# Loading q and k in runs of 32 features and transposing them on the vector engine, in a top-k attention with an MLP behind it

## The chip, the core and the metric

The kernel runs on one core of a Trainium2 chip. Its engines run side by side, each through its own queue in order: PE (TensorE, matmuls and transposes; PEld is its weight load), DVE (VectorE), ACT (ScalarE), POOL (GpSimd) and SP, which only issues DMAs here. The metric is the device time of one execution in microseconds, as the median of several runs. Lower is better.

## The reference

Eight batches of eight heads, 576 rows, 64 features: scores of every query against every key, of which only the 32 largest of a row are kept for a softmax; the result times v. The heads of one row side by side are the input x (4608 x 512) of an MLP with an exact GELU.

```python
scores = (1/sqrt(64)) * q @ k.T                   # per batch and head, 576 x 576
kth    = 32nd largest of each row
scores = where(scores >= kth, scores, -1e9)
attn   = exp(scores - max); attn /= attn.sum() + 1e-9
x      = (attn @ v) as (8*576, 8*64)
out    = gelu(x @ w_in) @ w_out                   # 512 -> 2048 -> 512
```

## The kernel before

**Pairs and items.** Two heads form a pair (`NP` = 4 pairs a batch, 32 in all). A pair's 576 rows are four blocks of 128 rows (`NM` = 4, `SM` = 512) and a tail of 64 (`TL`). An item is one block of a pair, both heads, or the tails of two pairs: 18 items a batch, 144 in all, in the order of the list `items`. The main loop `for n in range(ahead)` takes one step for each item and is written as a software pipeline by hand: in step n the scores of item n+2 are computed (`scores`), the largest 32 of item n are searched on DVE (`top_k`), the softmax of item n-1 runs on ACT (`softmax`), the probabilities of item n-2 are transposed on PE (`transposes`) and those of item n-3 multiplied by v (`attend`). The order of the text is the order of each engine's queue; nothing reorders it.

**A step on DVE.** `top_k` is eight MAX8 (line 344) and six MATCH_REPLACE8 (line 347) over 128 x 576. Then stands the hook `inverse(n - 1)`, the reciprocal of the softmax sums of the item before (line 370). It waits for `add_small` on POOL (line 376), which waits for the two softmax passes of ACT (lines 383, 384). Behind the reciprocal, POOL's `normalise` (line 396) scales the rows, and PE's `transposes` of that item (lines 415 to 433) come in the next step. In five steps around step 14 DVE takes over `normalise`.

**MLP.** Its matmuls (lines 522 and 558) are cut into pieces; a step takes at most eight (`left[0]`), from step `START` = 10 on. What is left runs behind the last item. Before `START`, `keep_busy` (line 636) fills PE with matmuls that nobody reads, and the weights (fp64 in memory) are loaded and converted unit by unit, one unit a step (`load_weights` on SP, `weights_size` on ACT, `weights_add` on POOL).

**q and k.** Scores need q and k with features on the partitions. `load` (lines 84 to 95) brings rows onto partitions: for each tensor of a pair two DMAs of 128 x 4 x 64 and two of 64 x 64, in runs of 64 features, 256 bytes. They go to SP's queue, but for k of pair 0 (ACT's and POOL's). There are two buffers for q and two for k. `transpose_qk` turns a pair: ten 128 x 128 transposes on PE (line 246) in three pieces of four, two and four, each piece into one PSUM tile `tp_qk` and from there by one copy on ACT into the tile `qk` (line 250; two of pair 0's copies are on DVE). The last piece issues the loads of the pair after next into the buffers that have come free. `slots_of` and `first` say in which step, counted from a batch's first, each piece of a pair is put; the pieces stand among PE's transposes and MLP pieces there. Pairs 0 and 1 are turned before the loop.

A tile `qk` holds q in columns 0 to 767 (512, then the tails of both heads on the diagonal of a block with zeros, then the same for k) and k behind them. There are six such buffers.

Of the kernel before, what the change touches and what calls it, by code (L numbers as in the profile page):

```python
# [14 lines left out]
def kernel(  # L15
# [52 lines left out]
    xT = const.tile([P, KO, RING], f32, name="xT")  # L68


    raws = {n: [const.tile([P, NJ, 2, D], f32, name=f"raw_{n}{i}") for i in range(m)]
            for n, m in (("k", 2), ("q", 2), ("v", NP + 1))}
    nc.gpsimd.memset(raws["k"][0][:, NM], 0.0)
    for t in raws["v"][:1] + raws["q"] + raws["k"][1:] + raws["v"][1:]:
        nc.vector.memset(t[:, NM], 0.0)


# [3 lines left out]
    def raw_of(n, pair):  # L81
        return raws[n][pair % len(raws[n])]

    def load(n, pair, queue=None, queue2=None):
        if pair >= n_pairs:
            return
        queue = queue or nc.sync
        queue2 = queue2 or queue
        b, h0 = pair // NP, 2 * (pair % NP)
        t, src = raw_of(n, pair), sources[n]  # L90
        for e in range(2):
            queue.dma_start(
                out=t[:, 0:NM, e, :], in_=src[b, h0 + e, 0:SM].rearrange("(t p) d -> p t d", p=P)
            )
            queue2.dma_start(out=t[e * TL : (e + 1) * TL, NM, e, :], in_=src[b, h0 + e, SM:S])

    load("k", 0, nc.scalar, nc.gpsimd)
    load("q", 0)
    make_identity(nc, ident)

# [127 lines left out]
    N = len(items)  # L228


    KT = SM + 2 * P
    qk_of = {}

    def transpose_qk(pair, first=False):

        rq, rk = raw_of("q", pair), raw_of("k", pair)
        blocks = [(rq, j) for j in range(NJ)] + [(rk, NM)] + [(rk, j) for j in range(NM)]

        def piece(c, n):
            if pair not in qk_of:  # L240
                qk_of[pair] = work.tile([P, KT + SM], f32, tag="qk", bufs=NP + 2, name="qk")
            t = qk_of[pair]
            tp = ps.tile([P, 512], f32, tag="tp", name="tp_qk")
            for x in range(n):
                r, j = blocks[c + x]
                nc.tensor.transpose(  # L246
                    tp[:, x * P : (x + 1) * P], r[:, j].rearrange("p e d -> p (e d)"), ident
                )
            copy = nc.vector.tensor_copy if first and c > 0 else nc.scalar.copy
            copy(out=t[:, c * P : (c + n) * P], in_=tp[:, 0 : n * P])  # L250
            if c == 0:
                load("q", pair + 2)
                load("k", pair + 2)

        return [lambda c=c, n=n: piece(c, n) for c, n in ((6, 4), (4, 2), (0, 4))]

# [18 lines left out]
    def scores(i):  # L277
        if i >= N:
            return
        pair, t = items[i]  # L280
        S_of[i] = s = work.tile([P, 2 * S], f32, tag="s", bufs=5, name="s")
        s_ps = ps.tile([P, 2, 512], f32, tag="s", bufs=1, name="s_ps")
        t_ps = ps.tile([P, 512], f32, tag="tp", name="t_ps")
        if t < NM:
            qk = qk_of[pair]
            lhsT = qk[:, t * P : (t + 1) * P]
            nc.tensor.matmul(t_ps[:, 0:P], lhsT=lhsT, rhs=qk[:, SM + P : KT], start=True, stop=True)  # L287
            for c in range(2):
                for e in range(2):
                    rows = slice(e * D, (e + 1) * D)  # L290
                    nc.tensor.matmul(  # L291
                        s_ps[:, e, c * 256 : (c + 1) * 256], lhsT=lhsT[rows, :],
                        rhs=qk[rows, KT + c * 256 : KT + (c + 1) * 256], start=True, stop=True,
                    )
            if i == 0:

                nc.scalar.activation(s[:, 0:SM], s_ps[:, 0], func=AF.Copy, scale=scale)  # L297
                nc.vector.tensor_scalar(s[:, SM : S + TL], t_ps[:, 0:P], scale, None, op0=ALU.mult)
                nc.scalar.activation(s[:, S + TL :], s_ps[:, 1], func=AF.Copy, scale=scale)  # L299
                return  # L300
            nc.scalar.activation(spread(s, S + TL, SM), s_ps, func=AF.Copy, scale=scale)  # L301
            nc.scalar.activation(s[:, SM : S + TL], t_ps[:, 0:P], func=AF.Copy, scale=scale)
        else:
            for r in range(2):
                qk = qk_of[pair + r]
                for e in range(2):
                    nc.tensor.matmul(
                        t_ps[half(r, e), r * TL : (r + 1) * TL],
                        lhsT=qk[:, SM + e * TL : SM + (e + 1) * TL],
                        rhs=qk[:, SM + P + e * TL : SM + P + (e + 1) * TL],  # L310
                        start=True, stop=True,
                    )

            for r in range(2):
                qk = qk_of[pair + r]
                for e in range(2):
                    rows = slice(e * D, (e + 1) * D)
                    nc.tensor.matmul(  # L318
                        s_ps[half(r, e), r, :], lhsT=qk[rows, SM + e * TL : SM + (e + 1) * TL],
                        rhs=qk[rows, KT:], start=True, stop=True,  # L320
                    )
            s2 = s.rearrange("p (r n) -> p r n", r=2)
            nc.scalar.activation(s2[:, :, 0:SM], s_ps, func=AF.Copy, scale=scale)
            nc.scalar.activation(
                s2[:, :, SM:S], t_ps[:, 0:P].rearrange("p (r n) -> p r n", r=2),
                func=AF.Copy, scale=scale,
            )
# [309 lines left out]

    keep_busy(WARM, idle)
    for pair in range(2):
        for piece in transpose_qk(pair, pair == 0):  # L640
            piece()
        if pair == 0:
            scores(0)
            scores(1)
# [1 line left out]


    slots_of = [
        [(-8, -7, -6), (-5, -4, -3), (-2, -1, 0), (1, 2, 3)],
        [(-10, -9, -8), (-7, -6, -5), (-4, -4, -3), (-3, -2, -2)],  # L650
    ]
    first = {2: (0, 1, 1), 3: (2, 2, 3)}
    prep_in = {}
    for pair in range(2, n_pairs):
        b, p = divmod(pair, NP)
# [3 lines left out]
    for n in range(ahead):  # L659

        left[0] = 4 if n in (START, START + 1) else 8
        eager[0] = n > N
        if not waits(unit_in(n)):
            weights_add(unit_in(n))
        scores(n + 2)
        product = attend(n - 3)
        late = n > START
        if n <= START:

            softmax(n - 1, 0)  # L670
        copy_x()
        if waits(unit_in(n)):
            weights_size(unit_in(n))
            weights_add(unit_in(n))
        mlp(1)
        tr = transposes(n - 2)
        if product and n > START and done[0] < len(pieces) and pieces[done[0]][0] > ready[0]:

            for piece in tr[:1]:
                piece()  # L680
            tr, ready[0] = tr[1:], n_tok[0]
        if n > START:
            softmax(n - 1, 0)
        mlp(1)
        if not late:
            softmax(n - 1, 1)
        mlp(1)
        if n < START:

            keep_busy((4 if product or n == 0 else 14) * (1 if n < 5 else 2), ident)  # L690
        prep = prep_in.pop(n, [])
        if n == START + 1:

            for piece in prep:
                piece()
            prep = []
        if len(prep) > 1 and len(tr) == 3:
            tr, prep = tr[:1] + prep[:1] + tr[1:], prep[1:]
        for piece in tr[:-1]:
            piece()  # L700
            if n < START and product and piece is tr[0]:
                keep_busy(5 if n < 5 else 10, ident)
            ready[0] = n_tok[0]
            mlp(1)
        ready[0] = n_tok[0]
        if late:
            softmax(n - 1, 1)
        add_small(n - 1)
        if ends_late(unit_in(n)):
            weights_end(unit_in(n))  # L710
        for piece in tr[-1:] + prep:
            piece()
            mlp(1)
        if n == 1:
            keep_busy(8, ident)

        run_gelus()
        mlp(left[0])
        run_gelus()
        if n < N:  # L720
            top_k(n, {3: lambda: inverse(n - 1)})
        else:
            inverse(n - 1)
        threshold(n)
        u = unit_in(n + 1)

        normalise(n - 1, 2 if on_pool(u) else 0)

        if not waits(unit_in(n + 1)):
            weights_size(unit_in(n + 1))  # L730
        for m in (n + 1, n + 2):

            if m > 2 and waits(unit_in(m)) == (m == n + 1):
                load_weights(m)
        if n <= NP:
            load("v", n)
# [38 lines left out]
```

## Time and profile before

| what | before |
|---|---|
| time, median of 3 runs (lowest, highest) | 1637.5 us (1636.53, 1637.75) |
| profiled execution: span from first to last instruction | 1634.7 us; what lies around it is not in the profile |
| PE / weight loads busy | 1611.5 / 1105.8 us |
| DVE / ACT / POOL busy | 1414.9 / 1185.3 / 665.3 us |
| mean granted TensorE clock | 0.999 |
| matmuls of `tp_qk` | 320, in the chain of work that ended last 2% |
| copies of `tp_qk` on ACT | 94, 48.3 us |
| idle time of DVE before the reciprocal | 134.4 us in 86 waits |
| idle time of DVE at the end | 73.7 us |
| DMA packets | 126768, of which 117776 under 512 bytes |
| load of q, 128 KB, issue to landing | 2.4 us (median of 64) |

Busy time is the time in which an engine worked on at least one instruction. In the lists of groups a line reads: source line, engine, operation, tile written and tiles read, shapes, count, then busy time in us and mean duration of one in ns, then the idle time of the engine just before them and what ended it. A mean duration on PE is longer than the distance from one matmul to the next, since matmuls overlap. In the table by stage each engine has its busy time and, in brackets, its instructions, and the last three columns are the granted clock, the busy share of the 16 DMA engines and GB/s.

### The profile page before, as it was taken

To read this page: it belongs to the slowest core of one execution; us is meant where nothing else is said; L and a number is where in the kernel's file an instruction comes from. 1 tells how busy PE (TensorE), PEld (TensorE's weight loads), DVE (VectorE), ACT (ScalarE), POOL (GpSimd) and SP (SyncE) were. 2 spreads that over 40 slices of the span, in tenths; PEclk is the share of its full clock that TensorE was granted. 3 is DMA by queue.
4 is the path that set the end of the run, shared out by engine and by line. 5 is a ranking of instruction groups with operands and counts; after the bars stand their busy time and mean duration, and the time that the engine had idled before them with its cause. 6 is when DMAs were issued, how large, how long until landed. Compare 5 with 4: busy or idle time off the path is not lost.

```text
span 1634.7 us, 25758 instructions
## 1 busy us (share of the span) xinstructions
PE 1611.5 (99%) x9184; PEld 1105.8 (68%) x9184; DVE 1414.9 (87%) x3046; ACT 1185.3 (73%) x2132; POOL 665.3 (41%) x760
## 2 busy tenths in 40 slices
PE   7999999999999999999999999999999999999999
PEld 5776676766666666666666667676666666666665
DVE  8999999988898899998899899998889889999800
ACT  6989877777777777777777777777777777777720
POOL 4986833333333333333333333333333333333300
PEclk9999999999999999999999999999999999999999
DMA  6523210011101120001110111001110101000000
GB/s 165 157 76 117 81 43 1 14 40 33 36 1 28 30 58 1 14 19 33 29 28 15 28 30 43 1 14 36 37 36 1 28 16 36 1 14 4 4 14 13
DMA packets 126768, 56.19 MB, mean 34 GB/s; under 512 B 117776, under 2 KB 118064, under 8 KB 126640
## 3 DMA queue, kind: packets, MB, share of 16 engines
q1 hardware_dynamic: 125376, 54.12, 12.3%
q8 instruction: 73, 1.20, 0.3%
q10 hardware_dynamic: 1200, 0.39, 0.1%
q14 instruction: 55, 0.45, 0.1%
q0 software_dynamic: 64, 0.03, 0.0%
HBM read 45.08 MB, written 9.44 MB: 33 GB/s over the span
## 4 chain that ended last, share of the span: by engine, by line
PE 91%; DVE 5%; ACT 2%; POOL 1%; issue 0%; SPq 0%; DMA 0%; DVEq 0%; POOLq 0%; ACTq 0%
PE h_ps L522 30%; PE y_ps L558 30%; PE o L470 8%; PE s_ps L291 7%; PE tp L433 7%; DVE top L344 3%; DVE rest L347 2%; PE tp_qk L246 2%; PE t_ps L287 2%; PE o L481 1%; PE tp_t L415 1%; PE s_ps L318 1%; POOL s L396 1%; ACT s L384 0%; ACT s L383 0%
## 5 line engine op out<-in xcount | busy, mean ns | idle before, releaser
L344 DVE MAX8 top<-rest 128x8 f32<-128x576 f32 x864 | 610.0, 748 | 0.0
L522 PE MATMUL h_ps<-xT,w_in_sb 128*128 128x256 f32 (+1 forms) x2560 | 553.1, 361 | 0.0
L558 PE MATMUL y_ps<-w_out_sb,g 128*128 128x512 f32 x1152 | 548.9, 599 | 0.0
L396 POOL TENSOR_SCALAR s<-s,rden 128x576 f32<-128x576 f32 x278 | 476.5, 1723 | 0.6 <-DVE rden L370 0.4
L522 PEld LDWEIGHTS h_ps<-xT,w_in_sb 128*128 128x128 f32 x2560 | 428.4, 191 | 61.8 <-issue 16.4
L347 DVE MATCH_REPLACE8 rest<-top,rest 128x576 f32<-128x576 f32 x576 | 423.7, 744 | 0.0
L376 POOL TENSOR_SCALAR den<-den 128x2 f32<-128x2 f32 x144 | 32.0, 222 | 826.5 <-ACT s L384 826.0
L558 PEld LDWEIGHTS y_ps<-w_out_sb,g 128*128 128x128 f32 x1152 | 195.1, 190 | 168.2 <-issue 167.3
L301 ACT ACTIVATE s<-s_ps 128x1024 f32<-128x1024 f32 x127 | 130.6, 1028 | 164.9 <-PE s_ps L291 143.4
L384 ACT ACTIVATE s<-s,bias 128x576 f32<-128x576 f32 x288 | 223.4, 776 | 13.2 <-ACT s L383 0.7
L383 ACT ACTIVATE s<-s,neg 128x576 f32<-128x576 f32 x288 | 224.2, 778 | 0.3 <-POOL neg L359 0.2
L440 ACT COPY pt<-tp 128x512 f32<-128x512 f32 x256 | 146.8, 575 | 99.7 <-PE tp L433 99.6
L347 DVE MATCH_REPLACE8 rest<-top,s 128x576 f32<-128x576 f32 x288 | 211.9, 744 | 0.0
L433 PEld LDWEIGHTS tp<-ident,s 128*128 128x128 f32 x1152 | 142.5, 141 | 89.7 <-issue 58.9
L344 DVE MAX8 top<-s 128x8 f32<-128x576 f32 x288 | 201.9, 743 | 1.4 <-ACT s L297 1.4
L433 PE MATMUL tp<-ident,s 128*128 128x128 f32 x1152 | 172.7, 273 | 4.6 <-ACT pt L416 4.3
L470 PE MATMUL o<-pt,raw_v 128*64 128x256 f32 x1280 | 152.7, 385 | 0.5 <-ACT pt L440 0.5
L291 PE MATMUL s_ps<-qk 64*128 64x256 f32 x1024 | 146.1, 404 | 0.8 <-ACT s L299 0.8
L370 DVE RECIPROCAL rden<-den 128x2 f32<-128x2 f32 x144 | 23.2, 161 | 134.7 <-POOL den L376 134.4
L470 PEld LDWEIGHTS o<-pt,raw_v 128*64 128x64 f32 x1280 | 86.4, 137 | 64.4 <-issue 21.4
L533 ACT ACTIVATE g<-h_ps 128x512 f32<-128x512 f32 x144 | 78.6, 595 | 37.8 <-PE h_ps L522 37.1
L291 PEld LDWEIGHTS s_ps<-qk 64*128 64x128 f32 x1024 | 88.6, 187 | 22.2 <-ACT s L299 1.0
(77 smaller groups left out, 1155.7 us busy)
## 6 DMA issues: line engine op xcount, KB each, us to landing
raw_q<-in_q_dram SPq DMA_DIRECT2D x64, 128.0 KB, 2.4
raw_v<-in_v_dram SPq DMA_DIRECT2D x64, 128.0 KB, 2.5
raw_k<-in_k_dram SPq DMA_DIRECT2D x62, 128.0 KB, 2.5
out_dram<-y SPq DMA_DIRECT2D x31, 256.0 KB, 2.2
w_out_sb<-in_moe_w_in_dram SPq DMA_DIRECT2D x14, 511.8 KB, 5.1
w_out_sb<-in_moe_w_out_dram SPq DMA_DIRECT2D x10, 511.8 KB, 4.2
words<-in_moe_w_out_dram SPq DMA_DIRECT2D x6, 511.8 KB, 4.2
out_dram<-y SPq DMA_DIRECT2D x9, 128.0 KB, 2.3
```

What stands on the lines that cost most here:

```text
L291: nc.tensor.matmul(s_ps[:, e, c * 256 : (c + 1) * 256], lhsT=lhsT[rows, :], rhs=qk[rows, KT + c * 256 : KT + (c + 1) * 256], start=True, s ...
L301: nc.scalar.activation(spread(s, S + TL, SM), s_ps, func=AF.Copy, scale=scale)
L344: nc.vector.max(st["top"][:, e, 8 * r : 8 * r + 8], cur[e])
L347: nc.vector.match_replace(rest[:, e], st["top"][:, e, 8 * r : 8 * r + 8], cur[e], LOWEST)
L383: nc.scalar.activation(s, s, func=AF.Prelu, bias=st["neg"][:, e, 1:2], scale=1.0, alpha=STEEP)
L384: nc.scalar.activation(s, s, func=AF.Exp, bias=st["bias"][:, e : e + 1], scale=1.0, accum_out=st["den"][:, e : e + 1],)
L396: (nc.vector if e >= 2 - on_dve else nc.gpsimd).tensor_scalar(s, s, st["rden"][:, e : e + 1], None, op0=ALU.mult)
L433: nc.tensor.transpose(tp[:, j * P : (j + 1) * P], s[:, first + j * P : first + (j + 1) * P], ident)
L440: nc.scalar.copy(out=dst, in_=tp.rearrange("p (j n) -> p j n", j=NM))
L470: nc.tensor.matmul(o[e * D : (e + 1) * D, 0:n], lhsT=vt[:, j, e, :], rhs=pt[:, e * NM + j if j < NM else 2 * NM, :], start=(j == 0), stop= ...
L522: nc.tensor.matmul(h_tile(u)[:, i, :], lhsT=w_in_sb[:, ko, f * P : (f + 1) * P], rhs=xT[:, ko, c0 : c0 + n], start=(ko == 0), stop=(ko == ...
L558: nc.tensor.matmul(y_of[sub], lhsT=g_of[u][:, i, sub * P : (sub + 1) * P], rhs=w_out_sb[:, f, :], start=(f == 0), stop=(f == FT - 1),)
```

## The change

The buffers of q and k become 128 x 640 tiles. `load` now puts 32 rows on 32 partitions, so that a run is 32 features of one row (128 bytes), and a square of 32 rows by 32 features lies where the transposed square has to be; the two heads and the two halves of the features take the four groups of 32 partitions. A tensor of a pair takes six DMAs (four large, two for the tails of the second head) in place of four. `transpose_qk` is one instruction on DVE for each tensor, which transposes every 32 x 32 square of the tile from SBUF to SBUF; each is followed by the load of the same tensor of the pair after next. `qk` has 640 columns of q and 640 of k. In the loop the two pieces of a pair stand in two steps (`slots_of`), behind the last search of the step and ahead of the reciprocal. Before the loop, those of pairs 0 and 1 stand ahead of the first search in DVE's queue. k of pair 0 is loaded from ACT's queue alone.

```diff
+    QK = SM + 2 * TL
+    SQ = 32
+    raws = {n: [const.tile([P, QK], f32, name=f"raw_{n}{i}") for i in range(2)] for n in "kq"}
...
+        if n != "v":
+            for e, a in ((0, 0), (0, 1), (1, 0), (1, 1)):
+                at = e * D + a * SQ
+                for lo, hi, c in ((0, S, 0),) if e == 0 else ((0, SM, 0), (SM, S, SM + TL)):
+                    (queue if a == 0 else queue2).dma_start(
+                        out=t[at : at + SQ, c : c + hi - lo].rearrange("p (j d) -> p j d", d=SQ),
+                        in_=src[b, h0 + e, lo:hi, a * SQ : (a + 1) * SQ].rearrange(
+                            "(j p) d -> p j d", p=SQ
+                        ),
+                    )
+            return
...
-    load("k", 0, nc.scalar, nc.gpsimd)
+    load("k", 0, nc.scalar)
...
-            tp = ps.tile([P, 512], f32, tag="tp", name="tp_qk")
-            for x in range(n):
-                r, j = blocks[c + x]
-                nc.tensor.transpose(
-                    tp[:, x * P : (x + 1) * P], r[:, j].rearrange("p e d -> p (e d)"), ident
-                )
-            copy = nc.vector.tensor_copy if first and c > 0 else nc.scalar.copy
-            copy(out=t[:, c * P : (c + n) * P], in_=tp[:, 0 : n * P])
-            if c == 0:
-                load("q", pair + 2)
-                load("k", pair + 2)
+                qk_of[pair] = work.tile([P, 2 * QK], f32, tag="qk", bufs=NP + 2, name="qk")
+            nc.vector.transpose(qk_of[pair][:, x * QK : (x + 1) * QK], raw_of(n, pair))
+            load(n, pair + 2)
-        return [lambda c=c, n=n: piece(c, n) for c, n in ((6, 4), (4, 2), (0, 4))]
+        return [lambda x=x, n=n: piece(x, n) for x, n in ((1, "k"), (0, "q"))]
...
-        [(-8, -7, -6), (-5, -4, -3), (-2, -1, 0), (1, 2, 3)],
-        [(-10, -9, -8), (-7, -6, -5), (-4, -4, -3), (-3, -2, -2)],
+        [(-8, -7), (-5, -4), (-2, -1), (1, 2)],
+        [(-10, -9), (-7, -6), (-4, -4), (-3, -2)],
-    first = {2: (0, 1, 1), 3: (2, 2, 3)}
+    first = {2: (0, 1), 3: (2, 3)}
...
-            top_k(n, {3: lambda: inverse(n - 1)})
+            def behind_searches():
+                for piece in prep_in.pop(n, []):
+                    piece()
+                inverse(n - 1)
+
+            top_k(n, {3: behind_searches})
```

## The prediction

> **What bounds the kernel now.** I read the busy times first, then the stages, the waits, and single steps in the timeline.
>
> ```profile
> PE 1611.5 (99%) x9184; PEld 1105.8 (68%) x9184; DVE 1414.9 (87%) x3046; ACT 1185.3 (73%) x2132; POOL 665.3 (41%) x760
> ```
>
> PE is nearly full and DVE is second. An average hides stages, so the table by stage (window, then PE, weight loads, DVE, ACT, POOL busy):
>
> ```profile
> 31.00:111.00 80.00, 71.22 (x557) 58.00 (x555) 80.00 (x173) 76.16 (x125) 73.89 (x59) 0.98 0.41 128
> 300.00:600.00 300.00, 300.00 (x1643) 202.84 (x1640) 270.44 (x582) 221.14 (x405) 111.56 (x137) 1.00 0.12 28
> 1560.00:1635.00 75.00, 71.08 (x250) 43.63 (x248) 0.42 (x1) 11.08 (x19) 1.05 (x1) 1.00 0.04 14
> ```
>
> Up to 111 us DVE has no gap: DVE sets the pace, PE fills up with warming matmuls. From about 125 us on PE has hardly a gap. The waits of DVE between 300 and 1560 us, and the reciprocal L370 in the first 111 us, say the same:
>
> ```profile
> DVE rden L370 <- POOL den L376: 124.3, 78, 8.7
> ...
> L370 DVE RECIPROCAL rden<-den x9: 148/162/165, 29.5 to 107.1; 128x2 f32<-128x2 f32 x9
> ```
>
> Early, nine reciprocals stand (107.1 - 29.5) / 8 = 9.70 us apart with no wait: the bare searches of one step. Later DVE waits at the reciprocal, at the end of each step, for the softmax sums of the step before, which ACT makes at PE's pace: 124.3 - 8.7 (the last, behind all searches) = 115.6 us over 117 steps, 0.99 us a step. PE waits for nobody in that window. What does one PE transpose cost there?
>
> ```profile
> 816.64 0.60 PE L246 MATMUL tp_qk<-ident,raw_q 128*128 128x128 f32 x4
> ...
> 817.08 1.45 PE L558 MATMUL y_ps<-w_out_sb,g 128*128 128x512 f32 x3
> 817.19 0.17 DVE L370 RECIPROCAL rden<-den 128x2 f32<-128x2 f32 x1 [0.55 <-POOL den L376]
> ```
>
> Four transposes start at 816.64, the next matmul at 817.08: 0.11 us each, not the 273 ns that a row gives for one (matmuls overlap). The groups that price the rest:
>
> ```profile
> L344 DVE MAX8 top<-rest 128x8 f32<-128x576 f32 x864 | 610.0, 748 | 0.0
> L396 DVE TENSOR_SCALAR s<-s,rden 128x576 f32<-128x576 f32 x10 | 4.8, 518 | 0.5
> L250 ACT COPY qk<-tp_qk 128x512 f32<-128x512 f32 (+1 forms) x94 | 48.3, 515 | 15.4 <-PE tp_qk L246 15.2
> ```
>
> **Removed.** 320 PE transposes and 96 copies. Those of pairs 0 to 4 fall where DVE sets the pace and PE has filler: worth nothing. The other 27 pairs: 270 x 0.11 = 29.7 us off a full PE. The copies, 48.3 us of ACT, lie beside PE's work (ACT 73% busy, PE waits for no qk copy after 300 us): nothing, either way.
>
> **Added on DVE.** Two transposes (T) of 128x640 for each pair, 64 in all. No row shows one. From below: the cheapest DVE pass from SBUF to SBUF, L396, 0.48 us for 576 columns, so 0.53 us for 640. From above: twice MAX8's rate, if a square had to be filled before it could be emptied. MAX8 is the nearest row (one pass over 128x576 fp32 in SBUF): two in 1.41 us in the timeline, 0.705 x 640 / 576 = 0.78 us, and double is 1.56. I take 0.78: every DVE row here stays between 0.8 and 1.3 ns a column.
>
> One rule weighed. The Trainium skill's page "VectorE: DVE Perf Modes", section "The three transpose paths", gives 311 ns for DVE on 128x128 bf16 and 390 ns for TensorE; five such blocks would be an estimate of 1.56 us a T, and a TensorE price of 390 ns would make the removal worth 105 us. The row for TensorE says 0.11 us here, so I trust the page's figures, which hold whole single instructions, in neither place; by the page's DVE figure the result would be that of the slow rival below.
>
> Where the T's lie. A T stands behind the last MAX8 of a step and ahead of the reciprocal, where DVE waits later on. From 300 us: 48 T's, 37 us, and PE's quicker pace takes another 240 x 0.11 = 26.4 us from the wait; of 115.6 us, 52 are left, 0.45 a step. A late reciprocal has further cover: at step 74 it stands at 817.19, the POOL normalise behind it ends some 4.0 us later, and PE's transposes of that tile start at 825.18, 4.0 us later (2.3 a step before). So from 300 us a T costs nothing; if DVE lost that cover, up to 37 us would return. Behind the waiting T nothing but the reciprocal and the next searches is queued on DVE.
>
> Before PE takes over there is no wait to hide in. T's of pairs 2, 3, 4 and the first of pair 5 run in steps 0, 1, 2, 3, 8, 9, 11: 7 x 0.78 = 5.5 us, in full. In steps 12 to 16 DVE also runs the ten normalisations of L396 (0.95 us a step) and five T's (3.9 us); its waits from 147 to 300 us are only 10.2 us in 15 steps. I charge 2.5 us (between 0 and 5).
>
> **The start.** The four T's of pairs 0 and 1 stand ahead of the first search. Before, pair 1 cost DVE nothing, and the first MAX8 ran at 10.21 us. Now it waits for q of pair 1. SP issues every 0.59 us (twelve from 0.72 to 7.22), and q0, k1 and q1 are 18 issues instead of 12: the last at 0.72 + 17 x 0.59 = 10.75, landing 2.4 us later, and 0.6 us more because the loads use eight landing semaphores in turn, and in the changed kernel's order the fifth and sixth load of k0 and q0 wait for earlier ones: 13.75. With T 14.5, so 4.3 us late (3.4 to 6.5). The packets: between 2 and 5 us 2685 packets take 101.3% of 16 engines, 18.1 ns each; runs of half the size are twice as many, and each lies between half of that and all of it. k0 and q0, 4608 packets, take 2.6 to 5.2 us against 2.6, under the queue's issue time.
>
> The page "DMA: Bandwidth & Descriptors", section "Why small descriptors are slow (HBM only)", speaks against the change: 3 cycles of overhead on each packet, 11 cycles for 256 bytes. An estimate by it is 7 for 128 bytes, 1.27 times the time for the same bytes; no run here shows it yet.
>
> Later loads have 20 us and more from a T to the next use of its buffer. SP blocks behind a T's release, as it did behind PE's (555.2 us of it), and v loads and stores stand behind; they have steps of room. Weights of slots 3 to 5 have less: six issues now stand ahead of them. Slot 5's is issued at 52.98, lands 4.2 us later, and is used at 57.81. I charge nothing: the step itself moves later, and the first sum is done 1.4 us ahead of its reciprocal (28.15 against 29.51 in the timeline).
>
> **Sum.** -29.7 + 5.5 + 2.5 + 4.3 = -17.4 us. The profiled span is 1634.7 us, the median of the runs 1637.5, and 2.8 us lie around the span and stay: span 1617.3, time 1620.1. The last 75 us have no T and no tp_qk and stay.
>
> **Rivals.**
> *T is slow, DVE takes over* (the slower side). At 1.56 us: start 5.1, seven early T's 10.9, steps 12 to 16 6, and from 300 us 75 us of T against 115.6 - 26.4 = 89 us of wait. The mean just fits, but two T's in neighbouring steps, 3.1 us, meet waits of 1.6 (124.3 / 78) and a cover of 2.3, and every second batch bunches four into three steps: some 2 us a batch, 12 in all. -29.7 + 5.1 + 10.9 + 6 + 12 = +4.3: 1641.8 us. It decides from T of about 1.4 us on. For it: nothing shows a T. Against: all DVE rows are quicker.
> *Loads late in the first 60 us.* If weights of slots 3 to 5 come 2 us late each, ACT stands with softmax behind it, and the sums come late: 6 us, 1626. For: ACT is 95% busy there. Against: ACT loses its copies.
> *PE sheds more.* The busy time of tp_qk from 111 us on is 43.3 us by the stages, not 29.7: 1606.5. Against: the starts in the timeline.
> That squares don't give the wanted layout is excluded: rows and features swap inside each square, and 32-feature runs put features on partitions.
>
> **How the numbers follow.** Forecast (1614 to 1624) 0.55; loads late 0.15; PE sheds more 0.08; T of 1.3 to 1.5 us, no difference, 0.06; T slower 0.16. A measurement here tells 0.2%, 3.3 us. Faster 0.78, same 0.06, slower 0.16. The range reaches from the third rival to the first: 1607 to 1642.
>
> **What would show it.** Right: T near 0.78 us; reciprocals of the T steps before 111 us 10.5 us apart; first MAX8 near 14.5; the wait at the reciprocal after 300 us about 50 us; PE still without gaps. Wrong: T over 1.3 us, PE waiting for POOL's normalise after 300 us, or a first search past 17 us.

## The result, and the profile after

The changed kernel takes 1622.6 us (median of 4 runs, 1621.96 to 1622.77) against 1637.55 for the kernel before: ratio 0.991, 95% interval 0.9898 to 0.9922. The forecast was 1620.1. Its profiled span is 1620.9 us, 13.8 us shorter than before.

The page of the changed kernel, busy times:

```profile
PE 1588.7 (98%) x8864; PEld 1082.8 (67%) x8864; DVE 1460.1 (90%) x3108; ACT 1144.1 (71%) x2038; POOL 663.9 (41%) x758
```

DVE is busy 45 us longer; PE is busy 23 us less, with the 320 transposes gone. The DVE transposes themselves, in the list of groups of the changed kernel:

```profile
L255 DVE STREAM_TRANSPOSE qk<-raw_k 128x640 f32<-128x640 f32 x32 | 26.5, 827 | 4.7 <-DMA raw_k<-in_k_dram 4.7
L255 DVE STREAM_TRANSPOSE qk<-raw_q 128x640 f32<-128x640 f32 x32 | 26.3, 822 | 2.2 <-DMA raw_q<-in_q_dram 2.2
```

One lasts 0.82 us from its own start to its own end. From its start to the next instruction's start it takes less, 0.73 to 0.75 us, as the steps show below; that distance is what it costs in a full queue. The idle times at the end of the lines are waits for loads, all in the first 13 us.

The start, from the timeline of the changed kernel: the last of the four transposes waits for q of pair 1, and the first search follows it. Before, that search began at 10.21 us.

```profile
12.39 0.85 DVE L255 STREAM_TRANSPOSE qk<-raw_q 128x640 f32<-128x640 f32 x1 [2.16 <-DMA raw_q<-in_q_dram]
13.16 1.38 DVE L347 MAX8 top<-s 128x8 f32<-128x576 f32 x2
```

The stages of the changed kernel (columns as in the table before) still show DVE without a gap from 31 to 111 us and PE without a gap from 300 us on. In the clock column there is something new, 0.74 and 0.91 in place of 1.00 and 0.98:

```profile
11.00:31.00 20.00, 14.84 (x82) 11.45 (x81) 18.61 (x38) 14.27 (x20) 5.43 (x5) 0.74 0.72 170
31.00:111.00 80.00, 70.27 (x528) 57.94 (x528) 80.00 (x173) 68.65 (x112) 68.73 (x56) 0.91 0.50 135
300.00:600.00 300.00, 300.00 (x1612) 201.27 (x1611) 289.25 (x615) 216.40 (x392) 117.90 (x145) 1.00 0.14 27
```

And the waits of DVE from 300 to 1560 us, which were 124.3 us in 78 waits:

```profile
DVE rden L373 <- POOL den L379: 67.5, 58, 8.7
```

The reciprocal at the end of each step is the mark by which the two kernels can be compared in time. The eighteenth, about where DVE stops setting the pace, from the timeline of the kernel before and then of the changed one:

```profile
204.75 0.17 DVE L370 RECIPROCAL rden<-den 128x2 f32<-128x2 f32 x1 [2.65 <-POOL den L376]
```
```profile
217.28 0.17 DVE L373 RECIPROCAL rden<-den 128x2 f32<-128x2 f32 x1 [3.73 <-POOL den L379]
```

There the changed kernel is 12.5 us behind. At the end it is 13.8 us ahead, so behind this point it has gained 26.3 us. These two numbers are what the experiments take apart.

### The profile page after: what moved, and what is told of

It reads as the page before. It is cut to its first block, busy times and chain, and to the rows that moved or that the text cites. A ratio compares the mean times of both kernels' runs of the same rounds, so it can differ in the third digit from the quotient of the medians.

```text
span 1620.9 us, 25358 instructions
## 1 busy us (share of the span) xinstructions
PE 1588.7 (98%) x8864; PEld 1082.8 (67%) x8864; DVE 1460.1 (90%) x3108; ACT 1144.1 (71%) x2038; POOL 663.9 (41%) x758
## 4 chain that ended last, share of the span: by engine, by line
PE 87%; DVE 10%; DMA 1%; SPq 1%; issue 0%; POOL 0%; ACT 0%; DVEq 0%; ACTq 0%; POOLq 0%
PE y_ps L561 30%; PE h_ps L525 30%; PE o L473 8%; PE s_ps L294 7%; PE tp L436 7%; DVE top L347 5%; DVE rest L350 4%; PE t_ps L290 2%; PE o L484 1%; PE tp_t L418 1%; PE s_ps L321 1%; SPq L99 1%; DVE qk L255 1%; DVE s L399 0%; PE t_ps L310 0%
## 5 line engine op out<-in xcount | busy, mean ns | idle before, releaser
L525 PE MATMUL h_ps<-xT,w_in_sb 128*128 128x256 f32 (+1 forms) x2560 | 547.5, 361 | 0.0
L561 PEld LDWEIGHTS y_ps<-w_out_sb,g 128*128 128x128 f32 x1152 | 198.8, 191 | 187.0 <-issue 186.2
L294 PE MATMUL s_ps<-qk 64*128 64x256 f32 x1024 | 150.8, 414 | 0.9 <-ACT s L302 0.5
L536 ACT ACTIVATE g<-h_ps 128x512 f32<-128x512 f32 x144 | 78.6, 594 | 37.8 <-PE h_ps L525 37.1
```

Source lines behind the costliest of these rows:

```text
L294: nc.tensor.matmul(s_ps[:, e, c * 256 : (c + 1) * 256], lhsT=lhsT[rows, :], rhs=qk[rows, KM + c * 256 : KM + (c + 1) * 256], start=True, s ...
L525: nc.tensor.matmul(h_tile(u)[:, i, :], lhsT=w_in_sb[:, ko, f * P : (f + 1) * P], rhs=xT[:, ko, c0 : c0 + n], start=(ko == 0), stop=(ko == ...
L561: nc.tensor.matmul(y_of[sub], lhsT=g_of[u][:, i, sub * P : (sub + 1) * P], rhs=w_out_sb[:, f, :], start=(f == 0), stop=(f == FT - 1),)
```

## The experiments

The pace theory: up to about step 17 DVE sets the pace and pays for every transpose; behind that PE does, and every PE transpose that is gone is 0.109 us. The rivals are in each expectation. Times are compared with the kernel before on the same chip (1637.4 and 1637.2 us) and with the changed one's 1622.6, beside which the kernel before took 1637.55.

**Pairs 0 to 7 the old way.** `qk` keeps the new layout; what PE turns is copied into it.

```diff
+    BY_PE = 8
-        if n != "v":
+        if n != "v" and pair >= BY_PE:
             for e, a in ((0, 0), (0, 1), (1, 0), (1, 1)):
...
+        if pair < BY_PE:
+            return [lambda c=c, n=n: by_pe(c, n) for c, n in ((6, 4), (4, 2), (0, 4))]
+        return [lambda x=x, n=n: by_dve(x, n) for x, n in ((1, "k"), (0, "q"))]
```

> Pairs 0 to 7 (all that are turned before 300 us) go the old way: 256-byte loads, PE transposes, ACT copies; pairs 8 to 31 as in the change. Pace theory (DVE sets the pace up to about step 17, PE behind it, and a DVE transpose costs its full time in the first part and nothing in the second): the 12.5 us by which the changed kernel is behind at step 18 go, the 26.2 us that 240 PE transposes free stay: 1637.55 - 26.2 = 1611.4 us. Rival, cost spread over the run (each of 64 transposes and its loads costs a little everywhere, a PE transpose frees its 0.16 us of busy time): a quarter of the 64 transposes goes back, so a quarter of both, and the time stays within 1619 to 1626.

Measured: 1611.36 us, ratio to before 0.9837 (0.9823 to 0.9852). This is the fastest of all versions, 11.2 us ahead of the change. Its stage from 300 us on:

```profile
300.00:1545.00 1245.00, 1244.90 (x6909) 841.40 (x6909) 1165.91 (x2484) 900.07 (x1630) 477.91 (x585) 1.00 0.11 23
```

PE has no gap there although DVE turns 24 pairs beside it. Its eighteenth reciprocal stands at 205.46 us, so of the 12.5 us lost in the early part all but 0.7 are given back. The gain of the late part stays, and the rival of a cost spread over the run falls.

**Each DVE transpose twice.**

```diff
-            nc.vector.transpose(qk_of[pair][:, x * QK : (x + 1) * QK], raw_of(n, pair))
+            for _ in range(2):
+                nc.vector.transpose(qk_of[pair][:, x * QK : (x + 1) * QK], raw_of(n, pair))
```

> Every DVE transpose is issued twice in a row, the second writing the same again. Pace theory: + 0.75 us for one of the four ahead of the first search, + 0.73 for each of the 12 up to step 16 (8.8 us), and behind step 28 48 more at 0.75 us against some 59 us of wait that is left at the reciprocals, bunched in pairs of neighbouring steps: 8 to 14 us. 1640 to 1646 us; up to step 18 the reciprocal is 9.5 us later than in the changed kernel. Rival, DVE has room for it everywhere: under 1633. Rival, DVE is already the bound behind 300 us: 64 x 0.75 = 48 us more, 1670.

Measured: 1652.47 us, slower than before (1.009, 1.0075 to 1.0105), and above the range expected. At the eighteenth reciprocal it is 23.2 us behind the kernel before, 10.7 more than the change (9.5 expected). The rest of the miss is late: of the 26.3 us only 7.4 are left, so 18.9 are lost where I expected 8 to 14. The waits of PE from 300 to 1560 us, of which the change has none:

```profile
PE tp_t L419 <- POOL s L400: 11.0, 12, 1.6
PE t_ps L311 <- DVE rden L374: 4.2, 3, 1.4
PE tp_t L424 <- POOL s L400: 1.4, 3, 0.5
```

Summed over the steps, DVE's wait would have covered the second transposes (37.8 us of it were still left there), but they do not always lie where a wait is. A late reciprocal makes `normalise` late, and PE's transposes of the probabilities then wait: these rows are 16.6 of the 18.9 us. About half of the loss comes in three bunches, where eight transposes stand in three neighbouring steps and the reciprocal falls back 2.9 us each time; the rest comes in single steps, most of them without a wait to hide in, 0.8 to 0.9 us each.

**PE transposes put back, unread:** ten for each of pairs 8 to 31, in pieces of 4, 2 and 4.

```diff
+    def unread(n):
+        tp = ps.tile([P, 512], f32, tag="tp", name="unread")
+        for x in range(n):
+            nc.tensor.transpose(tp[:, x * P : (x + 1) * P], ident, ident)
...
-        for piece in tr[-1:]:
+        for piece in tr[-1:] + pe_in.pop(n, []):
```

> The changed kernel with ten unread PE transposes of a constant for each of pairs 8 to 31, in the steps where the old ones stood; no ACT copies. Pace theory: what the change gains is the 0.109 us that each of 240 PE transposes took: + 26.2 us, 1648.8 us. Rival, the gain is ACT's 48 us of copies or the two PSUM buffers that tp_qk shared: no change, 1622.6.

Measured: 1648.86 us. 240 transposes cost 26.3 us, 0.109 us each, although no copy follows them. So the late gain of the change is PE's time. The two shared buffers are taken here too, but without the wait for a copy, so that part of the rival is only bounded: the first experiment gained 26.1 us in all with 24 pairs, copies included, which leaves nothing for copies or buffers.

**Runs of 32 features alone.** The kernel before, with only its loads changed.

```diff
+            for c in (slice(0, D),) if n == "v" else (slice(0, D // 2), slice(D // 2, D)):
+                queue.dma_start(
+                    out=t[:, 0:NM, e, c],
+                    in_=src[b, h0 + e, 0:SM, c].rearrange("(t p) d -> p t d", p=P),
+                )
```

> The kernel before with its four main loads of q and k of a pair cut in two of 32 features each (128-byte runs, 6 DMAs for a tensor instead of 4), PE transposes and copies as before. Pace theory: loads lie beside the work but for the first ones; k0 and q0 land up to 1.5 us later, so 1637.5 to 1639.5. Rival, small runs and their issues cost time by themselves: over 1642.

Measured: 1646.82 us, 9.4 us slower than before, and I had expected no more than 2. The rival is right in the amount, but not in the place. DVE's waits from 300 to 1560 us are 115.6 us, the same as in the kernel before once its last wait (8.7 us, behind all searches) is left out, so nothing is lost there. The first search begins 1.6 us late (11.79 against 10.21), about as expected, but the reciprocals are 5.7 us late at the first, 9.1 at the fifth (77.4 us) and 10.9 at the eighteenth, and stay there; the profiled spans differ by 10.9 us too. The longest wait of PE, from 11 to 300 us:

```profile
PE tp_qk L248 <- DMA raw_k<-in_k_dram: 6.3, 1, 6.3
```

This is k of pair 2, which PE turns in step 0. Its load stands on SP behind 24 issues for pairs 0 to 2 (six each for q of pair 0, k of pair 1, and q of pairs 1 and 2) and four for the first weights. Its first issue comes at 20.39 us in place of 13.11: there are eight issues more ahead of it, and the six of q of pair 2 take 7.1 us (13.27 to 20.34) behind those of the weights. PE, ACT and then DVE wait in turn; DVE waits 7.1 us in the first five steps that have a reciprocal, where it had no wait before. The changed kernel issues k of pair 2 ahead of q, and needs it only behind DVE's searches of step 0.

**Only pairs 0 and 1 the old way** (`BY_PE = 2`).

> Only pairs 0 and 1, whose four DVE transposes stand ahead of the first search, go the old way. Pace theory: the first search starts near 10.9 us as in the run with eight old pairs, instead of 13.16, and the rest is the changed kernel: 1622.6 - 2.3 = 1620.3 us. Rival, the late start is made up later (PE had slack to wait): 1622.6.

Measured: 1621.9 us, 0.7 us less than the change, though the first search begins at 10.37 us, 2.8 us earlier. In the list of groups of this run:

```profile
L261 DVE STREAM_TRANSPOSE qk<-raw_k 128x640 f32<-128x640 f32 x30 | 24.8, 827 | 2.3 <-DMA raw_k<-in_k_dram 2.3
```

DVE now waits 2.3 us behind step 0 for k of pair 2, the load that was late in the run before this one, and begins the second search at 23.18 us in place of 23.52. So the start is hardly shorter: what was freed turned into the next wait. The rest of the difference comes at step 18:

```profile
203.53 0.14 DVE L405 RECIPROCAL rden<-den 128x2 f32<-128x2 f32 x1
215.95 0.17 DVE L405 RECIPROCAL rden<-den 128x2 f32<-128x2 f32 x1 [2.65 <-POOL den L411]
```

That step lasts 12.42 us here and 13.51 in the changed kernel (203.77 to 217.28). In the step before it PE's clock is granted at half for 3.4 us here, and for 6.8 us there; the last experiment comes back to this.

**Pairs 0 to 4 the old way** (`BY_PE = 5`).

> Pairs 0 to 4 go the old way; pairs 5 to 7, in steps 11 to 16 where DVE also normalises, are turned by DVE. Pace theory: these six transposes and what they make late bring the 5.2 us by which the changed kernel falls back between steps 10 and 18: 1611.4 + 5.2 = 1616.6 us, and the 30 PE transposes of these pairs free nothing. Rival, PE sets the pace from step 11 on: then they are free and the 30 freed PE transposes gain 3.3 us over the run with eight: 1608.

Measured: 1615.55 us, 4.2 us above the run with eight old pairs, and 4.2 us is also the distance at the eighteenth reciprocal (209.65 against 205.46). So DVE still sets the pace through most of steps 11 to 16, and the six DVE transposes with the 30 PE transposes that they replace are a loss of 4.2 us. The six cost 4.4 at 0.73 each. There is a second cost beside them, which the expectation did not have: the ten normalisations on DVE take 7.1 us here, against 4.7 in the run with eight old pairs. The changed kernel has it too, 7.0 us against 4.8 before. One such step before, and then in the changed kernel:

```profile
136.50 0.95 DVE L396 TENSOR_SCALAR s<-s,rden 128x576 f32<-128x576 f32 x2
137.15 3.10 POOL L195 TENSOR_SCALAR w_out_sb<-w_out_sb 128x1024 int32<-128x1024 uint32 x1
```
```profile
180.16 2.94 POOL L210 TENSOR_SCALAR w_out_sb<-w_out_sb 128x1024 int32<-128x1024 uint32 x1
180.31 1.72 DVE L399 TENSOR_SCALAR s<-s,rden 128x576 f32<-128x576 f32 x2
```

A transpose between the last search and the reciprocal lets POOL's work on the weights begin ahead of the normalisations instead of behind the first. Against these 6.8 us DVE's waits between 111 us and the eighteenth reciprocal fell from 4.7 to 2.6, which leaves 4.7, near the 4.2. Whether the 30 freed PE transposes had a part in that is open; a net gain they did not bring.

**The transposes behind the reciprocal.**

```diff
             def behind_searches():
-                for piece in prep_in.pop(n, []):
-                    piece()
                 inverse(n - 1)
+                for piece in prep_in.pop(n, []):
+                    piece()
```

> The changed kernel with the DVE transposes of a step behind the reciprocal instead of ahead of it. Pace theory: what hides them after step 18 is DVE's mean slack, not their place in front of a wait: 1621.5 to 1623.6 us. Rival, only the wait ahead of the reciprocal hides them: each of 48 costs 0.75 us, 36 us more, 1658.

Measured: 1627.95 us, 5.4 us slower than the change. Neither case holds: the place matters, but far less than the rival says. PE's waits after 300 us in this run:

```profile
PE tp_t L418 <- POOL s L399: 2.9, 6, 0.5
PE tp_t L423 <- POOL s L399: 1.2, 3, 0.4
```

Long and short steps often alternate (9.7, 11.3, 9.7 and 11.4 us between the 22nd and the 26th reciprocal of the changed kernel): DVE waits in one and has no wait in the next. Behind the reciprocal the wait has passed unused, and the transpose lengthens the next step, which often has none. Most of the 48 transposes still cost nothing, which I put down to the time between a late reciprocal and PE's need of it; no run tests that alone. The profiled run is 6.4 us longer in its span than that of the change: 1.2 us are there at the twentieth reciprocal, and 5.2 come behind it, 4.1 of them as these waits of PE. Where the rest arises is not shown.

**A filler against the slow clock.**

```diff
+        if n == START + 7:
+            fill = ps.tile([P, 512], f32, tag="tp", name="fill")
+            for _ in range(26):
+                nc.tensor.matmul(fill[:, 0:P], lhsT=ident, rhs=ident, start=True, stop=True)
         scores(n + 2)
```

> The changed kernel with 26 unread matmuls of 128 columns at the start of step 17, where PE waits 2.9 us for the transposed q of pair 7 and the granted clock is 0.5 for 6.8 us behind that wait. Clock theory: the clock stays at 1.0, the scores and MLP matmuls there take 2.9 us less: 1619.7 us. Rival, PE is late there because of DVE and the slow spell is caught up in a later wait: 1622.6 us.

Measured: 1622.3 us, not to be told from 1622.6. The stretch from 185 to 200 us, of the changed kernel and then of this run (clock in the third column from the end):

```profile
185.00:200.00 15.00, 11.27 (x42) 5.68 (x41) 14.96 (x31) 8.80 (x16) 11.12 (x8) 0.77 0.29 86
```
```profile
185.00:200.00 15.00, 14.18 (x96) 10.74 (x95) 14.96 (x31) 9.21 (x17) 11.11 (x8) 1.00 0.30 89
```

The filler did keep the clock at 1.00. But it is no clean test, as PE's timeline shows, in this run and then in the changed kernel:

```profile
189.47 5.97 PE L671 MATMUL fill<-ident 128*128 128x128 f32 x52
195.37 0.45 PE L310 MATMUL t_ps<-qk 128*64 128x64 f32 x8
199.45 0.27 PE L418 MATMUL tp_t<-ident,s 128*128 128x128 f32 x1
```
```profile
192.48 0.48 PE L310 MATMUL t_ps<-qk 128*64 128x64 f32 x4 [2.90 <-DVE rden L373]
199.49 0.27 PE L418 MATMUL tp_t<-ident,s 128*128 128x128 f32 x1
```

The 26 matmuls stand as 52 records and took 5.97 us, 3.1 more than the wait that they were to fill. So the filler cost PE what the full clock gave back, and PE reaches the next `tp_t` at the same time. The equal times therefore say nothing for or against the clock theory. The run with two old pairs says more: its step 18 has a half-clock spell 3.4 us shorter ahead of it and is 1.1 us shorter, and in the changed kernel PE is busy from 203.8 to 217.3 us without a gap while DVE waits 3.73 us at the end of that step. So a part of the 12.5 us, of the order of 1 us, is the slow clock; no run isolates it.

## Why the prediction was right, point by point

- **What bounds it.** Right: DVE up to about step 17, PE afterwards with no wait from 300 us on. The wait of DVE that was left there, 67.5 - 8.7 = 58.8 us, was put at 52.
- **Price of a DVE transpose.** 0.78 us was worked out from MAX8. The first three reciprocals of the changed kernel stand (54.7 - 33.9) / 2 = 10.4 us apart, each with one transpose between them:

```profile
L373 DVE RECIPROCAL rden<-den x3: 122/122/123, 33.9 to 54.7; 128x2 f32<-128x2 f32 x3
```

  Early steps with one are 10.43 us long in place of 9.70, so 0.73, and late ones without a wait 10.47 against 9.72, 0.75. The estimate of 1.56 us, scaled from the Trainium skill's page "VectorE: DVE Perf Modes", section "The three transpose paths", was twice too high: the row decides.
- **The seven early transposes.** 5.5 us forecast, 7 x 0.73 = 5.1.
- **The start.** 4.3 us forecast, 2.95 measured (13.16 - 10.21). The mechanism was the one forecast, DVE waiting for q of pair 1. SP issued quicker than the 0.59 us I took from larger DMAs: the 18 issues run from 1.01 to 10.98 us, 0.55 each, with two waits of 1.0 us together for earlier landings among them (0.6 in the forecast). What was missed: without this delay the load of pair 2 would hold nearly the same place (the run with two old pairs).
- **Steps 12 to 16.** 2.5 us forecast; 12.5 - 2.95 - 5.1 = 4.4 measured. This is the term that was too small. The five transposes were priced about right (3.7 us at 0.75, 3.9 forecast). Two things were not in it: the normalisations on DVE became 2.2 us longer, and a half-clock spell of PE came into step 18, about 1 us. DVE's waits, which were to hide part, gave back only some 1 us (4.7 to 3.7 between 111 us and the eighteenth reciprocal). The early terms, 12.3 forecast against 12.5, were right in sum only: this error and those of the start and of the transposes met, which is luck.
- **Freed transposes.** Here is the step of the working that failed: PE was to set the pace from step 11 on, so 270 freed transposes were counted. The 30 of pairs 5 to 7 brought no net gain (the run with five old pairs). They are 3.3 us of the 3.6 by which the span's gain fell short, 13.8 against 17.4.
- **The late gain.** 240 x 0.109 = 26.2, measured 26.3. The transposes cost nothing there: right. The prediction gave three reasons: the place ahead of the wait, DVE's mean slack, and the time between a reciprocal and PE's need of it. The place is worth 5.4 us (the run with the transposes behind the reciprocal); mean slack alone is not enough (the run with each twice); the third is argued, not shown.
- **Slow transposes.** With two transposes for one, some 1.5 us, DVE has wait left on average, as the rival said, but the kernel loses more: 1652.5 us, where the rival had 1641.8. Its term that was too small is the stall in the late part, 18.9 us for its 12, and the gain against it was again 26.3 and not 29.7.
- **Loads late in the first 60 us.** Charged with nothing behind the start, rightly: ACT waits 3.1 us for weights before 130 us, but DVE, which sets the pace, is full from 31 to 111 us. Its 6.9 us of waits for loads all lie before its first search and are part of the start. That it turned out so depends on the order of the loads: the same runs in the order of the kernel before cost 9.4 us.
- **Packets.** Between 2 and 5 us the changed kernel has these queues:

```profile
DMA packets 4227, 0.52 MB, mean 175 GB/s; under 512 B 4227, under 2 KB 4227, under 8 KB 4227
...
q10 hardware_dynamic: 2259, 0.28, 59.0%
q1 hardware_dynamic: 1968, 0.24, 52.7%
```

  That is 111.7% of 16 engines over 3 us, 12.7 ns a packet against 18.1 in the kernel before, so 1.40 times the time for the same bytes. The estimate by the Trainium skill's page "DMA: Bandwidth & Descriptors", section "Why small descriptors are slow (HBM only)", was 1.27. Its direction agrees with the trace; the measured ratio is larger.

## What to carry to other kernels

Moving work from the full engine to the one with slack pays only in the stage where that engine is full; the same move cost 0.73 us an instruction and more in the first 200 us, where the other engine set the pace. Split such a change at that point: the version that keeps the old way for the first eight pairs is 26 us faster than before, the change everywhere 15. Where an engine waits in every second step, put the moved work in front of that wait, and count the matmul's start-to-start distance, not its duration, as what PE gets back.

## What the runs showed of the hardware that I had not expected

PE's clock was granted at half in spells of 3.4 us or a multiple, which begin in or at the end of PE's waits of 2.7 to 7.4 us: in the changed kernel from 192.1 to 198.9 us, where PE waited 2.9 us for the transposed q of pair 7, and in three spells before 60 us. With that wait filled the clock stayed at 1.00, so work that came late on DVE halved the clock of PE. The Trainium skill, page "TensorE: Matmul & The Clock Gate", part 1, tells of such a gate with two states and a window of about 3.4 us; the trace agrees in both.

A normalisation on DVE (TENSOR_SCALAR over 128 x 576) that began 0.15 to 0.29 us behind the start of POOL's pass over the weights took 1.2 to 1.4 us, in the changed kernel and in the runs with two and with five old pairs; those that began ahead of it, or more than 1 us behind, took 0.51 to 0.52. MAX8 beside the same pass kept its 1.41 us for two. The runs show the coincidence; none was made to test its cause.

A 32 x 32 transpose over 640 fp32 columns runs at the rate of a plain pass: 0.75 us, 1.17 ns a column, against 1.22 for MAX8.
